# A new step order for pooled attention and a gated feed-forward layer on one core

## The chip, the cores and the metric

The kernel runs on one core of a Trainium2 chip. The core has five engines that run their own streams of instructions and meet through semaphores: TensorE (matmul, with its weight loads apart), VectorE, ScalarE, GpSimd and SyncE, which here issues every DMA. The metric is the device time of one execution in microseconds (us). A short name for an engine in the profile: PE, PEld, DVE, ACT, POOL, SP in the order just given.

## The reference

Attention with pooled keys and values, then a gated feed-forward layer over all tokens. Batch is 8, heads 8, sequence 576, head size 64, so 4608 tokens of width 512; the inner width is 1536.

```
k_p, v_p = mean over 8 neighbours of k, v           # 576 -> 72
attn     = softmax(q k_p^T / 8)                      # 576 x 72 for each head
x        = attn v_p, heads side by side              # 4608 x 512
xn       = x / sqrt(mean(x*x) + 1e-6) * rms_g
out      = (silu(xn w_gate) * (xn w_val)) w_out      # 512 -> 1536 -> 512
```

## The kernel before

Weights come as 64-bit floats and are turned into a high and a low part, each of TensorE's float32r type; a product of two such pairs is three matmuls (high-high, low-high, high-low). Tokens are worked in 9 blocks of 512 (`NB`). Blocks 0 to 2 take plain products: for each of 12 slices `f` of the inner width a gate product, a value product (12 matmuls each), and the output product (12 matmuls). Blocks 3 to 8 go in pairs (3 and 4, 5 and 6, 7 and 8) through a seven-product scheme for 2 by 2 blocks: `product` (line 895) for the first layer and `product2` (line 975) for the second, 6 matmuls per step, with sums of blocks prepared by the other engines and partly stored to HBM and read back.

Nothing loops at run time and no scheduler reorders: with `manual_schedule`, each engine carries out its instructions in the order in which the program issues them, and `run` (line 1109) issues them by one long text, `ORDER` (line 52), of 3315 step names. So each engine's stream is that text with the other engines' steps left out. A name is a code of one or two letters (after `_` for the steps of batches 0 and 1 and of block 0) and indices; `:` gives PSUM banks for the step's results, `/` gives which of two or more buffers it takes. A capital first letter of some codes means the other one of VectorE and GpSimd (`_w`/`_W`, `wf`/`Wf`, `lo`/`Lo`, `fl`/`Fl`), or of VectorE and ScalarE (`_C`/`_D`, `_X`/`_Y`).

Steps that the text below names:

- `_S`, `sc` scores on TensorE; `_M` row maximum, `_E` exponentials, `_R` reciprocal, `_N` scaling of the probabilities on GpSimd (line 468); `_T` transposes of them on TensorE (line 536), `_D` or `_C` the copy out, `_A`, `av` probabilities times values
- `_P`, `_p`, `_r`, `_s`, `_B`, `_n`: squares summed on TensorE (line 652), total, root, its inverse, its spread over partitions (line 676), and the copy that scales block 0
- `_l`, `_a`, `_b`, `_c`, `_d`, `_h`, `_w`/`_W`: a weight's load, its conversion on ScalarE and VectorE, its high part (ScalarE), its low part. The low part on GpSimd goes through `cut` (line 292 in the profile), which makes pieces of 256 columns: 4 of them for a whole slice of the first layer, 2 for half of one or for a slice of the output weights
- block 0: `_m` and `_g`, `_e` the gate and value products, `_u`, `_G`, `_F` their scaling, silu and product, `_i` and `_j`/`_L` high and low part of it, `_o` the output product. `mg`, `me`, `gt`, `vl`, `hi`, `lo`/`Lo`, `mo` are the same for blocks 1 and 2
- `wt`, `wf`, `wh`, `wl`, `ws`: sums of weight blocks for the seven products, split and stored
- pairs: `ys`, `yh`, `yl`/`Yl` token sums and their two parts (`Yl` on GpSimd is 4 pieces), `rl` a weight load, `pr` a product; `fs`/`Fs`, `fh`, `fl`/`Fl`, `ft`, `pm` the same for the second layer

The order text was written by a planner that is not part of the file. It gave every step an engine, a place, banks and buffers.

Of the kernel before, what the change touches and what calls it, by code (L numbers as in the profile page):

```python
# [57 lines left out]
_C011 _E101 _N100 _T010:3 _T031 _v00 _V00 _A001:7/0 _Z01 _Y001 _x01 _D020 _b3 _b2 _c3 _c2 _d2 _h0 _y01 _T012:1 _W0
_A000:5 _Z00 _h2 _W2 _D012 _T032:6 _D010 _v01 _A020:4 _k11 _d3 _h3 _l4 _P00:2 _V01 _C032 _w3 _R101 _A021:1 _v10 _x20
_y20 _A010:3 _x00 _y00 _V10/0 _m000:7 _K11/1 _Y021 _x21 _y21 _Z21 _m010:6 _D031 _l7/0 _a7/1 _b7 _c7 _a4 _Z10 _ld/1 _l6  # L60
_ad/0 _m002 _b4 _Z20 _bd _A011:5 _Y011 _Z11 _d7 _x11 _A030 _x30 _Z30 _cd _c4 _x10 _dd _A031:4 _Z31 _P01 _P02 _P03 _a6
_hd _m012 _N101 _d4 _l9/0 _p _T100:1/1 _T101:2 _q11 _y30 _x31 _b6 _k12 _Wd _y11 _r0 _h7 _D101 _y31 _s0 _B00:5 _h4 _y10
_m011 _m001 _m013 _D100 _a9/0 _m003 _n _W4 _m100:5 Wt0/1 _l8 _Y031 _c6 _d6 _W7 _v11 _a8 _T102 _u0 _G0 _h6 _A100:1/1
_S11:27 _b9 _C102 _c9 _d9 _M110 _h9 _m102 _E110 _b8 _m110 _m112 _M111 _F0 _w9 _m101 _W6 _c8 _i0/1 _L0 Wf00 _d8 _lb/0
_R110 _m111 _K12/1 _A101:4 _ab/1 _X101 _bb _B01:6 _h8 _H01 _cb _m103 _u1 wf01 _db Wf02 _E111 _w8 _G1 _m113 _F1 wh03/0
Wl03 _la _X100 _hb _Wb _lf/0 Wf03 ws03 _e2:0 _o0:7564 _aa _g2:3 _i1/1 _ba _ca _L1 wh02/1 _o1 wl02 _af/0 _u2 _G2 _R111
_bf _cf _F2 _N110 _Q10 wd0 _i2/1 _T110:2/1 _D110 _df _hf _Wf _da _j2 _ha _g3:1 _lc _q12 _e3:0 wh01/0 _V11/0 _u3 _G3
# [5 lines left out]
ws21 _Wg _g6 _u6 _V12/0 _D122 _lk _k20 _v13 _o5 _G6 wh22/1 _F6 _i6/1 _ci _S13:10 _M130 _T120:3 _di wh24/0 Wl24 _D120
_j6 wl22 _M131 _g7 _u7 _hi ws22 _e7 _ak _o6 _K20/1 _bk _ck _G7 _F7 ws24 _E130 _dk _A121:3 _al/1 _bl _cl _ln/1 _an/0
_bn _cn _dl _i7/1 _R130 _dn _E131 _R131 _N131 _A120:2 _Y120 _hn _Wn _j7 _Y121 _g8:1 _u8 _V13/0 _G8 _wi _N130 wd4 _e8:0
_F8 _hl _wl _lj/0 _aj/0 _bj _cj _lm/1 _am/1 _bm _dj _T131:1/1 _o7 _D131 _hk _T130 _D130 _q20 sc20:21 wd2 _Q11/0 _cm
_T132 _D132 _dm _Wk _hj _A130:3 _Y130 Wt3/1 Wf30 _A131 _Y131 Wf31 lv21/0 mx201/1 sb201 _hm _Wj _wm _J11 mx200/1 lk21
pv21/0 _e9 sb200 wh33/0 Wl33 ex201 _lo/0 _i8/1 _L8 _g9:1 _u9 _ga:0 wh31/1 _o8 Wl31 ex200 _Q12/1 Wf32 Wf33 _J12 _Q13/0
ws33 _G9 _F9 ws31 _J13 _i9/0 wh34/0 pk21/1 Wl34 ws34 sm201/0 _ao/1 _bo _co _do _ho wh32/0 _L9 _P10:2 _ea _o9 _Wo _ua
sm200/0 nm200 _Ga _lp/0 _r1 Wl32 zd2 ws32 _Fa _ia/0 lq21 _ap/1 _gb:3 Nm201 tr20/1 _bp _La _s1 _B11:1 wd5 _cp _dp _hp  # L80
_ub _Gb _H11 wt4/0 _B10 _H10 _wp _eb:2 dm20 _Fb _oa sc21:10 wf40 wh41/0 Wl41 _t0 ws41 _t1 _ib/1 _jb wf41 wh43/1 _ob
lk22 Wl43 _t2 ws43 _t3 dp20/0 me10:2 Zt00/1 mg10:3 ev03/0 Wf42 Zt01 Zf00 Zf01 zh03/1 mx210/0 st03 sb210 Zl03 pk22/1
# [1127 lines left out]
```

## Time and profile before

| | us |
|---|---|
| median of 3 runs (lowest, highest) | 978.0 (974.93, 978.25) |
| the profiled execution's own time | 976.88 |
| span of the profile, first to last instruction | 975.1 |
| TensorE matmul busy | 947.5 (97%) |
| VectorE busy | 704.2 (72%) |
| ScalarE busy | 492.9 (51%) |
| GpSimd busy | 490.4 (50%) |

Busy time of TensorE counts a matmul that waits inside the pipeline as busy. The granted clock stands in shares of TensorE's full 2.4 GHz: 1.0 is that level, 0.5 is the level of 1.2 GHz. A row of the chain of waits follows the work that ended last back to the start.

### The profile page before, as it was taken

The page shows a single profiled execution, that of the slowest core. Times are in us where ns is not written, and L with a number is a line of the kernel's source. Part 1 is how long each engine was busy: PE and PEld are TensorE (multiplying, and loading weights), DVE is VectorE, ACT ScalarE, POOL GpSimd, SP SyncE. Part 2 cuts the span into 40 slices and gives each one's busy share as a digit, 9 for nine tenths or more (in the row PEclk, how much of TensorE's full clock was granted, in tenths as well). Part 3 has the DMA queues.
Part 4 walks back from the last instruction along what each step waited for, and adds up shares of the span by engine and source line. Part 5 has one row for each costly group of instructions (what it writes and reads, how often), then busy time and mean ns, then how long its engine had stood idle before and what let it go on. Part 6 is the DMA issues. An engine that isn't in the chain of part 4 may idle for free.

```text
span 975.1 us, 14181 instructions
## 1 busy us (share of the span) xinstructions
PE 947.5 (97%) x4670; PEld 752.2 (77%) x4670; DVE 704.2 (72%) x1134; ACT 492.9 (51%) x929; POOL 490.4 (50%) x618
## 2 busy tenths in 40 slices
PE   7799999999999999999999999999999999999997
PEld 6577677777777877877877777877877778888885
DVE  6989898978787888778787877755565884433333
ACT  5876675645555647555455456242543642213332
POOL 3355637222322324433455788432296894445785
PEclk7789999999999999999999999999999999999999
DMA  9537774665766569878887776768686465767646
GB/s 300 183 137 273 225 247 157 215 204 178 240 204 204 171 182 267 251 231 274 253 248 255 202 253 195 243 184 263 217 257 212 155 219 173 229 189 232 205 141 204
DMA packets 142296, 211.41 MB, mean 217 GB/s; under 512 B 12240, under 2 KB 78288, under 8 KB 140944
## 3 DMA queue, kind: packets, MB, share of 16 engines
q1 hardware_dynamic: 142224, 210.52, 68.8%
q8 instruction: 37, 0.61, 0.3%
q14 instruction: 35, 0.29, 0.1%
HBM read 154.24 MB, written 56.23 MB: 216 GB/s over the span
## 4 chain that ended last, share of the span: by engine, by line
PE 76%; DMA 5%; DVE 5%; POOL 5%; ACT 3%; issue 2%; SPq 1%; DVEq 0%; ACTq 0%; POOLq 0%
PE pxy L895 30%; PE psg L1059 15%; PE pf L975 15%; PE po L1093 7%; PE psx L560 3%; PE pss L478 3%; POOL w L292 2%; DMA pt<-rows 1%; DMA ring<-vs 1%; POOL xp L292 1%; POOL hl L292 1%; DMA ring<-vB 1%; DVE wt L326 1%; PE psr L652 1%; DVE wt L330 1%
## 5 line engine op out<-in xcount | busy, mean ns | idle before, releaser
L895 PE MATMUL pxy<-xp,wp 128*128 128x512 f32 x1512 | 361.1, 391 | 1.5 <-ACT o L1104 0.7
L895 PEld LDWEIGHTS pxy<-xp,wp 128*128 128x128 f32 x1512 | 282.3, 188 | 65.3 <-issue 2.5
L975 PE MATMUL pf<-fp,ring 128*128 128x512 f32 x756 | 189.8, 393 | 3.1 <-DMA ring<-vB 1.6
L1059 PE MATMUL psg<-xh,w 128*128 128x512 f32 x544 | 171.2, 396 | 1.4 <-DVE prob L495 1.0
L975 PEld LDWEIGHTS pf<-fp,ring 128*128 128x128 f32 x756 | 139.6, 188 | 39.6 <-DMA ring<-vs 3.9
L1059 PEld LDWEIGHTS psg<-xh,w 128*128 128x128 f32 x544 | 101.2, 189 | 26.5 <-DVE prob L495 1.4
L1059 PE MATMUL psg<-xl,w 128*128 128x512 f32 x272 | 106.7, 392 | 0.0
L292 POOL TENSOR_TENSOR hl<-act,hh 128x256 fp32r<-128x256 f32 x58 | 49.8, 878 | 111.5 <-ACT hh L1075 102.6
L292 POOL TENSOR_TENSOR fp<-fs,fp 128x256 fp32r<-128x256 f32 x108 | 81.1, 778 | 41.7 <-ACT fp L948 37.9
L292 POOL TENSOR_TENSOR fp<-act,fp 128x256 fp32r<-128x256 f32 x72 | 55.1, 786 | 83.1 <-ACT fp L948 81.8
L1093 PE MATMUL po<-w,hh 128*128 128x512 f32 x288 | 72.9, 390 | 0.0
L292 POOL TENSOR_TENSOR w<-wt,w 128x256 fp32r<-128x256 f32 x50 | 48.7, 1000 | 45.7 <-ACT w L344 45.7
L1093 PEld LDWEIGHTS po<-w,hh 128*128 128x128 f32 x288 | 54.1, 188 | 11.6
L292 POOL TENSOR_TENSOR fp<-hb,fp 128x256 fp32r<-128x256 f32 x68 | 54.5, 828 | 13.9 <-ACT fp L948 13.9
L1059 PEld LDWEIGHTS psg<-xl,w 128*128 128x128 f32 x272 | 51.4, 189 | 11.1
L1154 ACT COPY hb<-pxy 128x512 f32<-128x512 f32 x36 | 21.0, 586 | 72.7 <-PE pxy L895 72.7
L1161 DVE TENSOR_TENSOR u<-u,pxy 128x512 f32<-128x512 f32 x36 | 24.7, 685 | 38.0 <-PE pxy L895 37.8
L948 ACT CAST fp<-act 128x512 fp32r<-128x512 f32 x36 | 22.2, 619 | 58.5 <-DVE act L1162 49.3
L948 ACT CAST fp<-fs 128x512 fp32r<-128x512 f32 x54 | 33.0, 618 | 34.3 <-POOL fs L292 16.7
L1155 DVE TENSOR_TENSOR u<-hb,pxy 128x512 f32<-128x512 f32 x36 | 24.6, 684 | 33.3 <-PE pxy L895 19.7
L292 POOL TENSOR_TENSOR fs<-act,hb 128x256 f32<-128x256 f32 x32 | 23.4, 752 | 50.0 <-DVE act L1162 28.0
L1158 DVE TENSOR_TENSOR hb<-u,pxy 128x512 f32<-128x512 f32 x36 | 24.7, 686 | 29.0 <-PE pxy L895 28.1
(193 smaller groups left out, 1636.0 us busy)
## 6 DMA issues: line engine op xcount, KB each, us to landing
wp<-sum SPq DMA_DIRECT2D x144, 256.0 KB
wp<-blocks SPq DMA_DIRECT2D x108, 256.0 KB
ring<-vs SPq DMA_DIRECT2D x72, 256.0 KB
ring<-vB SPq DMA_DIRECT2D x54, 256.0 KB
sum<-wt SPq DMA_DIRECT2D x48, 256.0 KB
blocks<-w SPq DMA_DIRECT2D x24, 512.0 KB
wx<-w SPq DMA_DIRECT2D x10, 1024.0 KB
v<-vN SPq DMA_DIRECT2D x32, 288.0 KB
```

The source lines that it names most:

```text
L292: getattr(eng, op)(*(x[..., o:o + step] for x in (out, a, b)))
L478: nc.tensor.matmul(s["ps", h][:, t * SP:(t + 1) * SP], s["q"][r, o:o + P], s["pk"][r, :], start=True, stop=True)
L560: nc.tensor.matmul(ps[r, :n], s["pv"][:, r], x, start=True, stop=True)
L895: nc.tensor.matmul(ps[:, :NB], w[:, a, c, :], x[:, b, c, :], start=j == 0 and not more, stop=j == len(todo) - 1, skip_group_check=more)
L948: nc.scalar.copy(y[:, 0], f_source(i, k, j))
L975: nc.tensor.matmul(ps[c], w[:, a, c * P:(c + 1) * P], x[:, b], start=j == 0 and n == 0 and not more, stop=j == HALF - 1 and n == 2, skip_g ...
L1059: nc.tensor.matmul(ps[:, :NB], w[:, c, cols], x[c], start=(j == 0), stop=(j == len(todo) - 1))
L1093: nc.tensor.matmul(po[i][t], x[i, f][:, t * P:(t + 1) * P], w, start=(f == 0 and k == 0), stop=(f == NF - 1 and k == 2))
L1154: cp=lambda i, f: S_.copy(later(i, f), st["XY", i, f, 0]),
L1155: u2=lambda i, f: V.tensor_add(u2(i, f), later(i, f), st["XY", i, f, 1]),
L1158: c2=lambda i, f: V.tensor_sub(later(i, f), u3(i, f), st["XY", i, f, 4]),
L1161: v1=lambda i, f: V.tensor_add(u2(i, f), u2(i, f), st["XY", i, f, 5]),
```

## The change

Only the text `ORDER` is another one. It holds the same 3315 steps; the functions, tiles and shapes stay as they are. The plan behind it keeps the pieces that GpSimd makes of one instruction next to each other, and has no piece without a duration. The places of most steps move by a few, banks and buffers are given anew, and 48 steps change their engine: GpSimd has 300 steps for 309, VectorE 1016 for 1006, ScalarE 695 for 696. TensorE has the same 640, and SyncE the same 675.

The stretch of the text around `_T121` as it was, and as it is:

```diff
-wh11/1 wl11 _ce _de _A110:1 _v20/1 _V20/1 _Y110 ws11 _o3 _A111:1 wh13/0 wd1 _i4/0 Wt2/1 _E120 _g5:0 wh14/1 _R120 Wl14
-ws14 Wf20 _li Wl13 _L4 ws13 _ag _o4 _bg _e6 _he _We Wf21 _u5 _cg _E121 _R121 _dg wf22 _N121 wh12/1 Wl12 _e5:2 ws12 _G5
...
+_bg ws13 _e6 _j4 Wf22 _cg _u5 _o4 _G5 _dg _N121 _hg _F5 _i5/0 _T121:1/1 _j5 _g6:0 wh23/0 Wl23 _We _li _ai ws21 wh22/1
```

GpSimd's own stream there, read out of the two texts:

```
before: N111 wl01 _Wc _Wh wf13 wl11 _L4 _We wf22 _N121 _N120 _Wg wl22
after:  N111 _Wa wf12 wf13 _Wc wl11 _N120 wl21 _N121 _We wl22 _Wg _L6
```

TensorE's own stream, from the third output product of block 0:

```
before: _o2 _g4 _T112 _T111 _e4 _S12 _A110 _o3 _A111 _g5 _o4 _e6 _e5 _T121 _T122 _g6 _o5
after:  _o2 _T110 _T112 _T111 _g4 _A110 _S12 _A111 _e4 _g5 _o3 _e5 _e6 _o4 _T121 _g6 _T122 _o5
```

And earlier, from the first: before `_m103 _m113 _e2 _o0 _g2 _o1`, after `_m103 _g2 _m113 _o0 _e2 _o1`; GpSimd's low parts of weights ahead of it: before `_W4 _W7 _W6 _L0`, after `_W6 _W7 _W4 _W9 _L1`. ScalarE's high part `_h7` stood ahead of `_G0` and stands behind it.

## Rows read from the trace of the kernel before

**Rows 1.** The page, parts 1 and 2: busy time by engine, and TensorE's busy share and granted clock in 40 equal slices.
```profile
PE 947.5 (97%) x4670; PEld 752.2 (77%) x4670; DVE 704.2 (72%) x1134; ACT 492.9 (51%) x929; POOL 490.4 (50%) x618
PE   7799999999999999999999999999999999999997
PEclk7789999999999999999999999999999999999999
```

**Rows 2.** Busy time by stretch: us from the span's start, then PE, PEld, DVE, ACT and POOL busy (instructions), granted clock, DMA share, GB/s.
```profile
0.00:25.00 25.00, 18.67 (x147) 16.97 (x148) 17.46 (x41) 14.52 (x63) 7.53 (x19) 0.73 0.90 297
25.00:50.00 25.00, 19.99 (x103) 13.64 (x101) 21.84 (x36) 22.27 (x62) 10.38 (x13) 0.77 0.58 193
50.00:100.00 50.00, 47.59 (x242) 37.29 (x243) 45.30 (x64) 32.86 (x68) 30.43 (x30) 0.94 0.56 198
100.00:200.00 100.00, 96.30 (x493) 75.68 (x492) 89.84 (x147) 67.64 (x151) 47.80 (x51) 0.98 0.67 211
200.00:300.00 100.00, 100.00 (x540) 78.01 (x539) 85.27 (x164) 53.59 (x101) 25.16 (x34) 1.00 0.67 206
900.00:976.00 76.00, 69.91 (x303) 55.75 (x301) 29.39 (x40) 22.47 (x39) 54.51 (x75) 0.99 0.57 184
```

**Rows 3.** The same view in stretches of 5 us.
```profile
45.00:50.00 5.00, 5.00 (x29) 4.71 (x25) 3.83 (x5) 4.98 (x10) 1.57 (x2) 0.58 0.78 235
50.00:55.00 5.00, 5.00 (x22) 4.35 (x22) 3.59 (x9) 1.21 (x4) 0.10 (x1) 0.50 0.69 256
...
110.00:115.00 5.00, 3.89 (x18) 2.88 (x16) 4.47 (x6) 3.37 (x9) 5.00 (x4) 1.00 0.64 244
115.00:120.00 5.00, 3.85 (x14) 2.97 (x15) 4.17 (x7) 3.30 (x6) 1.72 (x3) 0.75 0.83 261
120.00:125.00 5.00, 5.00 (x31) 3.93 (x31) 3.64 (x5) 2.43 (x6) 3.57 (x5) 0.91 0.99 371
150.00:155.00 5.00, 3.97 (x18) 2.98 (x17) 4.47 (x8) 3.22 (x6) 4.13 (x6) 1.00 0.04 8
```

**Rows 4.** The chain of work that ended last, around 110 us: start, us, what.
```profile
108.87 4.78 POOL w L292 x4
...
114.15 0.90 POOL wsum L766
115.05 1.69 POOL prob L468 x2
...
116.78 0.41 PE pst L536 x2
117.19 4.35 PE psg L1059 x12
```

**Rows 5.** TensorE in order of time: start, us, line, operation, tiles, count, and the idle time before with what ended it.
```profile
113.50 0.39 PE L1059 MATMUL psg<-xl,w 128*128 128x512 f32 x1
115.85 0.63 PE L536 MATMUL pst<-ident,prob 128*72 128x128 f32 x4 [1.96 <-POOL prob L468]
116.78 0.41 PE L536 MATMUL pst<-ident,prob 128*72 128x128 f32 x2 [0.30 <-POOL prob L468]
```

**Rows 6.** GpSimd in order of time, same columns.
```profile
56.21 9.98 POOL L292 TENSOR_TENSOR w<-wt,w 128x256 fp32r<-128x256 f32 x10 [6.10 <-ACT w L344]
...
108.87 5.32 POOL L292 TENSOR_TENSOR w<-wt,w 128x256 fp32r<-128x256 f32 x4 [3.03 <-ACT w L344]
...
120.49 2.82 POOL L292 TENSOR_TENSOR w<-wt,w 128x256 fp32r<-128x256 f32 x4 [3.77 <-ACT w L344]
123.36 0.74 POOL L775 TENSOR_TENSOR wt<-wsum,wt 128x256 fp32r<-128x256 f32 x1
```

**Rows 7.** VectorE in order of time: the two reciprocals (`_R120`, `_R121`) that the scalings `_N120` and `_N121` wait for.
```profile
107.54 0.18 DVE L463 RECIPROCAL early<-early 128x5 f32<-128x5 f32 x1
...
111.84 0.18 DVE L463 RECIPROCAL early<-early 128x5 f32<-128x5 f32 x1
```

**Rows 8.** ScalarE in order of time: the silu `_G0`, a high part of a whole slice of the first layer, and of half of one.
```profile
60.11 0.63 ACT L1037 ACTIVATE act<-act 128x512 f32<-128x512 f32 x1
60.65 1.03 ACT L344 CAST w<-wt 128x1024 fp32r<-128x1024 f32 x1
62.72 0.62 ACT L344 CAST w<-wt 128x512 fp32r<-128x512 f32 x1 [1.04 <-DVE wt L330]
```

**Rows 9.** The chain of work that ended last, in the start-up, and one stretch of plain products at the full clock.
```profile
45.36 6.01 PE psr L652 x30
...
54.57 1.84 PE psb L676 x10
...
299.20 10.88 PE psg L1059 x48
```

**Rows 10.** Groups of ScalarE's instructions: busy us, mean ns | idle before.
```profile
L499 ACT ACT_TABLE_LOAD x26 | 33.4, 1283 | 0.5
```

**Rows 11.** In order of time, at the start of the second pair: GpSimd's `Yl53`, then `Yl54` and `Yl55`, and TensorE's product that reads `Yl54`'s result.
```profile
592.84 2.83 POOL L292 TENSOR_TENSOR xp<-xs_S,xp 128x256 fp32r<-128x256 f32 x4 [1.45 <-ACT xp L861]
...
598.73 7.00 POOL L292 TENSOR_TENSOR xp<-xs_S,xp 128x256 fp32r<-128x256 f32 x8 [1.69 <-ACT xp L861]
...
602.10 1.55 PE L895 MATMUL pxy<-xp,wp 128*128 128x512 f32 x6
```

**Rows 12.** The end of the chain of work that ended last.
```profile
957.03 4.02 DMA ring<-vB
...
970.59 1.37 DVE fu L1005 x2
```

More of the change, by code (lines that the diff above doesn't have):

```diff
@@ L58 @@
[L58 to L67, printed above, removed]
@@ L73 @@
[L73 to L82, printed above, removed]
@@ L158 @@
-Fl341 rl510/5 lq70 pr3b6 v13b va3b rm60:3 rt60 rc60 ft341 rs60 pm341 ft342 pm342 rl502/6 ys53/10 ys54 rl503/7 pr510:3
-Fs345 ft344 pr500 Fl344 fh335/4 Fl335 fh325/7 Fl325 ft343 pm343 ft345 cp50 pr502 fh350/8 rl512/0 ft325 ft335 pm325
-Fs365 pm344 cp51 rl521/4 pm335 rl501/6 rl511/3 Fl350 ft350 qc30 yh53 qc31 sa50 Yl53 fh345/5 qe31/1 qe30/0 Fl345 pr512
-sc70:75 oe31 yh52 yl52 fh352/3 fl352 yh54 ft352 pm350:26 Yl54 sa51 pm345 ft351 pm351 ys55 yh55 mx701/1 sb701 mx700/0
-rl504/2 pr504:4 lk72 ft353 fh353/5 sb700 pk72/0 Yl55 pm352 ex701 pr501:5 Qd31 u250 pr511 u251 sm701/1 fh363/6 pr503:7
@@ new lines @@
+_C030 _h2 _D011 _W2 _T031:1 _D031 _d3 _A021:4 _Y021 _v01 _V01 _x20 _h3 _P00:2 _y01 _y00 _y20 _T032:7 _C032 _A011:5
+_ld/1 _ad/0 _W3 _k11 _K11/0 _bd _m010:6 _m000:7 _l4 _x21 _y21 _v10 _m012 _cd _a4 _b4 _Z21 _Y001 _dd _R101 _Y011 _N101
+_x11 _l7/0 _a7/1 _b7 _c7 _Z20 _c4 _hd _A031:3 _Z31 _A010:4 _A030:1 _x30 _Z30 _P02 _Z10 _d7 _l6 _P03 _y11 _Z11 _P01 _d4
+_R100 _N100 _x10 _a6 _x31 _b6 _y30 _p _m002 _r0 _T100:5/1 _T102 _c6 _y10 _V10/1 _Wd _s0 _h4 _d6 _D102 _l9/0 _T101:2
+_l8 _a9/0 _b9 _Y031 _y31 _m001 _D101 _k12 _c9 _d9 _B00 _h6 _n _m011 _m003 _u0 _a8 _W6 _G0 _m013 Wt0/1 _B01:2 _H01
@@ new lines @@
+_S11:37 _M110 _M111 _m100:0 _K12/0 _h7 _lb/0 _la wd0 _b8 _m110:2 _m102 _D100 _A100:5/1 _E110 _A101:1 Wf00 _k13 _W7 _F0
+_c8 _d8 _X100 _m112 _q12 _i0/1 _j0 _m101 _m111 _ab/1 _bb _m103 _u1 _cb Wf01 _db _W4 _g2:3 _h9 _W9 _E111 _h8 Wf02 _m113
+wh03/0 Wl03 _w8 _G1 _o0:7465 _F1 _aa _lf/0 _i1/0 _L1 _ba _ca ws03 _Y101 _af/0 _bf _e2:0 _u2 _cf _lc _hb _Wb _R110 _df
+wh02/1 _da _G2 _F2 _v11 _hf _Wf _i2/1 _o1 Wl02 _L2 ws02 _g3:1 _e3:0 _lh/0 _ac wh01/0 wl01 ws01 _R111 _V11/1 Wf03 _ha
+_o2 _K13/1 _u3 _G3 _bc _cc _F3 _N110 _T110/0 _ah/1 wh04/0 _bh _ch _dc _dh _N111 _T112:3 _D110 _le _T111:1 Wl04 _Wa
@@ new lines @@
+Wt1/0 _i3/0 _j3 Wf10 _D112 _D111 _g4:0 _u4 _v12 _A110:1 _hh Wf11 wf12 _Y110 _v20/1 _S12:23 _wh _ae _A111:1 _e4:0 _Y111
+_M120 _M121 _be _ce wf13 _hc _g5:1 _Wc _G4 _F4 ws04 wh11/0 wl11 _lg wh14/1 Wl14 ws14 _V20/1 _E120 _R120 _N120 _o3
+_V12/0 Wt2/1 _de _Q11/0 _E121 _R121 ws11 wh12/1 Wl12 ws12 Wf20 _i4/1 Wf21 _e5:2 wh13/0 _ag _he Wl13 _q13 wh21/1 wl21
+_bg ws13 _e6 _j4 Wf22 _cg _u5 _o4 _G5 _dg _N121 _hg _F5 _i5/0 _T121:1/1 _j5 _g6:0 wh23/0 Wl23 _We _li _ai ws21 wh22/1
+Wf23 _u6 _G6 _T122:2 _o5 _bi wl22 _lk _D122 _F6 _Wg _k20 _C121 ws23 _ci _T120:2 wh24/0 ws22 Wl24 _D120 _K20/0 _i6/1
@@ new lines @@
+_L6 _Q10 _J11 _S13:10 _ll/0 _M131 _A121:3 _X121 _di _ak _al/1 _hi _g7 _u7 _bk _G7 _M130 _bl _cl ws24 _o6 _ln/1 _an/0
+_bn _cn _E130 _Wi _dn _e7:2 _A120:3 _Y120 _g8:1 _dl _v13 _F7 _i7/0 _L7 _ck _e8:2 _dk _u8 _E131 _R131 _N131 _R130 _lm/1
+_V13/0 _hn _wn _o7 _G8 _T131/1 _hl _F8 _wl _lj/0 _aj/0 _bj _cj _q20 _N130 _T130:1 _am/1 _bm _D131 _T132:3 _dj _hj _cm
+_dm _i8/0 lv21/0 _D130 _D132 zd3 Wt3/1 Wf30 _hm sc20:02 mx201/0 _A130:1 _Y130 _Wm _wj _A131:3 _hk lk21 pv21/0 _L8
+_Q12/1 Wf31 wh31/1 _g9:1 _Y131 _lo/0 _e9 wh33/0 Wl31 ws31 _Q13/0 Wf32 Wf33 Wl33 _u9 _G9 mx200/1 _o8 sb200 _F9 _Wk ws33
@@ new lines @@
+cp50 Fl325 pr502 ft344 ft345 fh335/4 Fl335 Fs365 yh53 Fl345 ft325 pm325 pm344 ys54 sa50 qe31/1 ft335 qe30/0 pm335 qc31
+fh365/7 qc30 yh52 yh54 rl510/5 pr510:3 cp51 ft352 yl52 pm345 sc70:75 fh350/5 Yl53 fh352/3 oe31 ys55 yh55 pr512 sa51
+rl513/7 rl505/4 mx701/0 mx700/0 pr504:4 rl501/5 sb701 sb700 ft350 ft351 Fl350 pm350:26 pm351 lk72 pk72/0 fh361/5 oe30
+Yl54 ex701 pr501:5 ft353 fh353/6 fl352 pm352 ft354 Qd31 qf31/1 pr511 rl520/6 rl503/2 rl521/3 u250 Yl55 pr503:5 u350
+lv70/0 c250 rl514/0 fh354/8 u251 Fl353 pm353 ft361 pr505:7 v250 Qd30 qf30/0 ys56 Fl354 lq71 fh355/4 Fl355 pm354
@@ new lines @@
+sc73:10 Jn71 Fs532 mx730/1 mx731/0 sb731 qb50 rl595/2 rl593/0 av720:3 xc720 sq72/0 Fs540 pr593:6 Fl531 sb730 rl596/4
+ft521 rl592/7 pr592 u359 pr595:0 c259 v259 ft522 rl5b4/3 rl5a0/1 pr5a0:3 lv73/1 pv73/1 fh532/8 rl5a3/0 ex730 pr596
+rl5b1/7 sm730/1 pr5a3:6 Fl521 Nm730 fh522/7 Fl522 ex731 sm731/1 sw59 vb59 pm521 Fs561 Fl532 Fs562 rl5a1/2 pr5a1:7
+ft530 v159 rl5a6/4 pm522 cp5a rl5a2/5 pr5a2 rl5a4/6 Nm731 Fs533 sa5a u25a u35a pr5a4:6 Jn72 fh533/7 tr73/0 c25a
+rl5b0/1 rl5a5/2 pr5a5:1 Fs543 sa59 v25a pm530 rl5b3/5 dm73 ft523 fh543/4 sw5a va59 Fl533 Fs563 pr5a6 ft524 ft532
@@ L227 @@
+Fl762 fh754/8 Fl754 fl753 pm753 Qd70 fh760/7 qf70/1 pm754 Fl760 qc71 Qd71 qf71/0 ft761 pm760 fh761/6 ft762 ft764
+fh763/5 pm755 ft763 qg71 og71 of71 Fl761 pm761 pm762 of70 fs765 Fs764 fh764/4 Fl763 pm763 Fl764 qg70 ft765 pm764 og70
+fh765/3 Fl765 pm765 qh71 oh71 qh70 oh70
 """
```

288 lines of the change are left out of this document (141 added, 147 removed).

## Prediction

> **What bounds the kernel now.** I read the page first: TensorE is busy 947.5 of 975.1 us, every other engine at most 72%, and the granted clock is below full only in the first two of the forty slices [rows 1]. So TensorE's own work is the bound, and a new order can only touch what TensorE idles and what it does at half clock. The busy time by stretch says where that is [rows 2]: the idle time is 25.00 - 18.67 = 6.3 us up to 25, 5.0 up to 50, 2.4 up to 100, 3.7 up to 200 and none up to 300. From 900 to 975.1 it is 75.1 - 69.9 = 5.2, of which 975.1 - 970.59 = 4.5 follow the last sum's start [rows 12]. The whole is 27.6, so 300 to 900 holds the other 27.6 - 22.6 = 5.0. From 120 us on an order can win no more than these 5.0, some 0.7 ahead of the tail, and the 3.7 less the 1.11 and 1.15 idle from 110 to 120 [rows 3], together 7; the rest is the start.
>
> Then I took the same view in short stretches and the chain [rows 3, 4]. Two places stand out. From 45.4 to 55 the engine is busy, at a clock of 0.50 to 0.58: thirty of the small sums of squares take 6.01 us [rows 9]. At 115 the chain leaves TensorE, goes through GpSimd (four pieces, `_We`; then 0.90, `wf22`; then two scalings in 1.69), and comes back at the transposes `_T121` and `_T122` [rows 4]. TensorE waits 1.96 and 0.30 us there for the scalings [rows 5], and the granted clock falls from 1.00 to 0.75 in that stretch [rows 3]. The next gate product takes 4.35 us [rows 4], where 48 matmuls of the kind at full clock take 10.88 us, so 12 take 2.72 [rows 9].
>
> **The change part by part.** *The stall at `_T121`.* Its reciprocal was done at 111.84 + 0.18 = 112.0 [rows 7], and yet the scaling `_N121` began at 115.05 [rows 4], because `_We` (108.87 to 114.2, beginning late by a wait for its high part [rows 6]) and `wf22` were ahead of it on GpSimd. In the new order `_N120`, `wl21`, `_N121` stand ahead of `_We`, and `wf22` has gone to VectorE. The set of TensorE's steps ahead of `_T121` is the same, so TensorE comes there at about the same time: 113.50 + 0.39 = 113.9 [rows 5]. What it finds hangs on `wl21`, a new wait in front of `_N121`: it takes 0.74 [rows 6], and needs a high part on ScalarE that now stands behind some whole-slice conversions of about 1.03 each [rows 8]. Queued behind it on GpSimd are `_N121`, `_We` and `wl22`, and TensorE's `_T121` waits for the first. With `_N120` begun behind its reciprocal (107.72) and 1.69 / 2 = 0.85 a scaling, `_N121` could end at 112.0 + 0.85 = 112.9; with two of those conversions and `wl21` in front, at 112.9 + 2.06 = 115.0. The first removes the whole stall: 1.96 + 0.30 and the half-clock loss 4.35 - 2.72 = 1.63, together 3.9 us. The second leaves a wait of 1.1 and probably part of the clock loss. Below nothing it could go if the high part came later still, but then the wait is the one of today. I take 3.4, near the better end, as VectorE has six steps fewer ahead of `_R121` and these run at 0.75 us each or so (4.47 for 6 in 110 to 115 [rows 3]). The bounds are 0 and 3.9. `_We` now ends later, about 113 + 5.3; its readers stand behind `_g6` as before, in products that run past 120.
>
> *The start, up to 60 us.* The order of some forty steps of VectorE and ScalarE changes. Both are the bound there: 21.84 and 22.27 of the 25 us from 25 to 50 [rows 2]. Counted in the two texts, 87 VectorE steps stand ahead of `_F0`, the first finished slice, where there were 85; at the mean of that stretch, 21.84 / 36 = 0.61, that is up to 1.2 us more. But the ones taken out are larger than those put in by their shapes (two copies to the transposed attention and a cast, for three short copies, a set of pooled keys and a sum), so I take +0.5. ScalarE exchanges `_h7` (half a slice, 0.62 [rows 8]) and three copies for `_h6` (1.03) and three others ahead of `_G0`, about +0.2. Later slices come some tenths earlier, as `_F1` and `_F4` have less VectorE work ahead. I put the start at 0, with bounds -1 and +3; the half-clock stretch is the reason for a wider one, and a rival.
>
> *The low parts of `_g2`'s weights.* On GpSimd `_W4` and `_W6` change places. Ten pieces took 9.98 us from 56.21 [rows 6]. Before, `_W4` was the first four, over by 60.2; now it is the last four, over at 66.2 if the ten start as before. `_g2` stands one product earlier on TensorE, at about 66.7 by my walk along the order. So the cover is half a us: I count nothing, and a rival below pays for it. `_W9` comes onto GpSimd ahead of the low part `_L1` (two pieces, 2 us at that pace).
>
> *150 to 155.* `_e9` and `_g9` change places where TensorE idles 5.00 - 3.97 = 1.03 [rows 3]; it lies between 0 and 1.0 of gain, and I take 0, as what both wait for is the same weight and state of VectorE and ScalarE.
>
> *The pairs.* `Yl53` ends at 592.84 + 2.83; `Yl54` and `Yl55` follow at 598.73 for 7.00, and the product that reads `Yl54` starts at 602.10, just as its half is there (598.73 + 3.50 = 602.2) [rows 11]. In the new order that product stands one product earlier, and GpSimd has a low part `Fl` ahead of `Yl53` and one between it and `Yl54`. Gain 0, loss up to three such products, 3 x 1.55 = 4.7; I take 0, since GpSimd idles 1.45 and 1.69 there, about what the added parts of four pieces in 2.8 take.
>
> *Edits with no price of their own.* From 200 to 300 TensorE idles nothing, with VectorE at 85.27, ScalarE at 53.59 and GpSimd at 25.16 of 100 us [rows 2]: the engine changes of single steps are covered there. Each switch of ScalarE's table costs 1.283 us [rows 10]; counted along the text there are 83 for 80, so 3.8 us more, on an engine that is half idle [rows 1]. Banks and buffers: their first users stand at about the same distance. The tail has the same four products last, behind the same read-back of 4.02 us [rows 12], and stays.
>
> *A rule against the change.* The same four-piece operation took 5.32 us at 108.87 and 2.82 at 120.49 [rows 6], the first beside a VectorE busy 4.47 of 5 us, the second beside 3.64 [rows 3]. The Trainium skill, "GPSIMD Engine Reference", section "8. Key points", says that GpSimd shares its SBUF interfaces with VectorE and is held up by VectorE instructions in certain modes or with two SBUF inputs. The rows agree with that as far as they go. By the rule, pieces set next to each other slip by up to 5.32 - 2.82 = 2.5 us per group where VectorE is dense; by the rows alone they may slip or not, and the sum keeps its values. That is behind the second and third rivals.
>
> *The sum.* The profiled execution took 976.88 by its own time, 1.8 over its span. Start 0, `_T121` -3.4, the rest 0: 973.5. The median of the runs is 978.0, 1.1 above that execution; so the forecast is 974.6.
>
> **The rivals.**
>
> *More is won.* The stretch at half clock, 45.4 to 55.4, holds nearly 10 us, of which at full clock up to 5 would be left. If the earlier sums of squares come closer to the other work ahead of them, part of it runs at full clock; 3.4 for `_T121` and 4.6 here give 978.0 - 8 = 970. For it: the step order there is altered, and the clock has two levels, so it goes by jumps. Against it: these sums stand behind VectorE's and ScalarE's copies, which are no shorter.
>
> *Nothing changes in sum.* The stall at `_T121` goes, and `_e5`, `_T122` or the `Yl` stretch meets it again: low parts slip by one group's 2.5 us plus 1 us, 978.0 - 3.4 + 3.4 = 978. For it: at 602 the margin was 0.1 us; after 113 `_We` is late by as much as `_N121` is early. Against it: TensorE never idles from 200 to 300 in the same density.
>
> *Slower.* `_W4` comes last of GpSimd's ten pieces while `_g2` comes earlier. Behind `_W6`, `_W7` waits for `_h7`, which now stands behind `_G0` (60.11 + 0.63, then 0.62 [rows 8]: ready at 61.4 at the earliest); when that slips with the start, `_W4` slips with it. Then TensorE waits at 66.7 and the chain moves on to `_L1` behind `_W9`. A slip of 4.5 and two fallings of the clock at 1.7 each (1.63 at `_T121`) cost 7.9; with `_T121`'s 3.4 kept, 978.0 + 7.9 - 3.4 = 982.5. It decides from where `_W4` ends beyond 66.7 + 1.7 = 68.4. For it: half a us of cover. Against it: `_W6`'s high part needs only VectorE steps that come no later, and four of the ten pieces may run at 0.7 us.
>
> *The change does not do what it says.* If most order moves are covered, and `wl21`'s wait is as long as `_We`'s was, the time is 978.0 again; this is inside the second case.
>
> **How the numbers follow.** The forecast has 0.42, more gain 0.24 (around 970), nothing in sum 0.18 (around 978), slower 0.16 (982.5 and above). A difference of 0.5%, 4.9 us, is about what a measurement of this kernel can tell from no change: faster means below 973.1, slower above 982.9. The forecast lies 1.5 inside the bound, so about a third of its chance (0.14) is faster, and all of the gain case: 0.38. Of the slower case and the other cases' upper ends 0.16 lies above. The rest, 0.46, is between. The range: below, the gain case to its middle and 2 further, 968; above, the slower case just beyond its price, 983. The forecast's own range takes in `_T121`'s bounds and the start's better one: 974.6 - 0.5 - 1.0 to 974.6 + 3.4, 973 to 978.
>
> **What would show it.** For `_T121`: the wait for the scaling ahead of its transposes below 0.5 us, a granted clock of 1.00 from 115 to 120, and the gate product after it at 2.7. For the start: the first plain products at the same place within a us, the thirty sums of squares in 6.0 us. For `_W4`: no idle time with a GpSimd low part as its releaser between 64 and 72. For the pairs: no wait of a product for `xp` from GpSimd at about 600. The prediction is wrong if the half-clock stretch before 60 us grows or shrinks by more than 2 us, if a wait of over 2 us for a GpSimd piece appears anywhere, or if `_T121` still waits.

## The result, and the profile after

The changed kernel takes 981.9 us in the median of 13 runs (979.5 to 989.1), the kernel before 977.4 (974.5 to 981.0). Over all runs the ratio is 1.0053 (that of the medians is 1.0046), with an interval of 1.0035 to 1.0070. It became about 5 us slower where 3.4 less were forecast; 981.9 lies inside the range, at its upper end, with the wrong sign. The profiled execution took 980.02 us by its own time, 3.1 more than that of before.

The five longest of the 13 runs (983.2 to 989.1, 986.0 in the mean) have a granted clock of 0.976 to 0.978, the other eight (980.7 in the mean, 3.3 above the kernel before) one of 0.980 to 0.984. By these clocks, 0.977 and 0.982 in the mean, the five were granted some 0.005 x 980 = 5 us less of TensorE's full clock; that estimate is about their whole distance of 5.3. The trace below is of one of the eight and doesn't show where they lose it.

Busy time and granted clock on the page of the changed kernel, as in [rows 1]:

```profile
PE 947.0 (97%) x4670; PEld 748.5 (77%) x4670; DVE 712.6 (73%) x1144; ACT 497.9 (51%) x931; POOL 500.7 (51%) x611
PE   7898999999999999999999999999999999999997
PEclk7799999999999999999999999999999999999999
```

TensorE is busy as long as before, so the difference between the two traces is idle time. Where it lies is read from the busy time by stretch, with the columns of [rows 2] and [rows 3]:

```profile
80.00:100.00 20.00, 18.52 (x102) 14.14 (x101) 19.21 (x27) 13.52 (x29) 16.29 (x16) 1.00 0.59 201
100.00:110.00 10.00, 8.63 (x39) 6.81 (x37) 8.47 (x13) 6.74 (x24) 6.30 (x4) 1.00 0.45 142
110.00:115.00 5.00, 4.69 (x23) 3.86 (x24) 4.10 (x6) 2.22 (x4) 4.75 (x4) 1.00 0.66 245
115.00:120.00 5.00, 4.43 (x21) 3.40 (x20) 4.23 (x7) 3.87 (x7) 3.40 (x5) 1.00 0.88 328
140.00:160.00 20.00, 17.93 (x101) 13.93 (x100) 19.52 (x31) 13.30 (x25) 12.27 (x13) 1.00 0.61 188
...
300.00:900.00 600.00, 593.60 (x2845) 472.97 (x2844) 418.75 (x653) 282.47 (x452) 307.22 (x390) 1.00 0.74 224
900.00:978.00 78.00, 70.36 (x304) 56.14 (x302) 29.30 (x39) 21.57 (x38) 54.26 (x73) 1.00 0.56 174
```

From 110 to 120 TensorE idles 0.88 us where it idled 1.11 + 1.15, and the clock is 1.00 where it was 0.75 [rows 3]. But from 80 to 110 it now idles 1.48 + 1.37 = 2.85, and nothing in that stretch before:

```profile
80.00:100.00 20.00, 20.00 (x108) 16.06 (x108) 19.39 (x25) 11.54 (x18) 12.36 (x12) 1.00 0.75 271
100.00:110.00 10.00, 10.00 (x45) 7.49 (x44) 9.93 (x15) 8.41 (x28) 5.64 (x7) 1.00 0.65 188
```

VectorE, nearly full there before (19.39 + 9.93 = 29.3 of 30 us), is busy 27.7 now. From 140 to 160 TensorE idles 2.07, where 150 to 155 had 1.03 [rows 3]. From 300 to 900 it is 6.4 for 5.0, and from 900 to the end at 977.9 it is 77.9 - 70.4 = 7.5 for 5.2 [rows 2]. The same for the changed kernel in TensorE's order of time, only instructions from 75 us on with idle time ahead of them, and what ended it (columns of [rows 5]):

```profile
75.69 0.73 PE L1093 MATMUL po<-w,hl 128*128 128x512 f32 x2 [0.93 <-POOL hl L292]
86.97 1.25 PE L536 MATMUL pst<-ident,prob 128*72 128x128 f32 x10 [0.56 <-POOL prob L468]
94.72 0.73 PE L1059 MATMUL psg<-xh,w 128*128 128x512 f32 x2 [0.90 <-DVE act L1033]
110.31 1.20 PE L1093 MATMUL po<-w,hl 128*128 128x512 f32 x4 [1.68 <-DVE hl L292]
117.31 1.19 PE L1093 MATMUL po<-w,hl 128*128 128x512 f32 x4 [0.57 <-DVE hl L292]
142.29 0.85 PE L536 MATMUL pst<-ident,prob 128*72 128x128 f32 x6 [0.57 <-POOL prob L468]
145.89 1.19 PE L560 MATMUL psx<-pt,pv 72*64 72x288 f32 x8 [1.48 <-ACT pt L542]
...
592.55 1.65 PE L895 MATMUL pxy<-xp,wp 128*128 128x512 f32 x6 [1.54 <-ACT act L1156]
...
956.59 11.57 PE L975 MATMUL pf<-fp,ring 128*128 128x512 f32 x48 [1.76 <-DMA ring<-vs]
```

The first of these rows, in `_o1`, is no new wait (0.93 before too), but a place to compare: it stands at 75.69 to 77.01 in the eight traces with the changed order up to there, and at 77.21 to 80.33 in six with the order of before. So the changed kernel leads at this row and loses the lead behind it; and one order alone spreads over 3 us here, so that the lead of a single trace says little.

The 1.96 at `_T121` [rows 5] is gone. The 1.68 at 110.31 stands in its place: `_o4` waits for `_j4`, the low part that was on GpSimd as `_L4` and is on VectorE now. Two of GpSimd's rows and the chain of waits tell why `_j4` is late; first GpSimd in order of time:

```profile
101.44 3.93 POOL L775 TENSOR_TENSOR wt<-wsum,wt 128x256 fp32r<-128x256 f32 x1
...
111.15 1.77 POOL L468 TENSOR_TENSOR prob<-prob,early 128x360 f32<-128x360 f32 x1
```

and the chain that ended last (start, us, what):

```profile
101.48 3.90 POOL wt L775
...
105.40 2.02 DMA sum<-wt
...
107.49 0.41 ACT wt L771
107.90 0.49 ACT wt L318
...
108.83 1.04 ACT w L344
109.87 0.32 ACT wt L771
```

`wl11`, an instruction of 0.74 us elsewhere [rows 6], takes 3.9. Its store lands 2.0 later and frees the buffer for `wh13` on ScalarE (L771); `Wl13` on VectorE waits for `wh13`, and `_bg` and `_j4` stand behind `Wl13`. Behind `wh13` on ScalarE come `_ag`, `_he` and `wh21`, and for `wh21` the `wl21` that the change puts ahead of `_N121`. The prediction had seen that last wait alone. The row at 592.55 is new as well, and comes back below.

### The profile page after: what moved, and what is told of

It is laid out like the page before. It is cut to its first block, busy times and chain, and to the rows that moved or that the text cites. A ratio compares the mean times of both kernels' runs of the same rounds, so it can differ in the third digit from the quotient of the medians.

```text
span 977.9 us, 14177 instructions
## 1 busy us (share of the span) xinstructions
PE 947.0 (97%) x4670; PEld 748.5 (77%) x4670; DVE 712.6 (73%) x1144; ACT 497.9 (51%) x931; POOL 500.7 (51%) x611
## 4 chain that ended last, share of the span: by engine, by line
PE 72%; DVE 6%; DMA 6%; POOL 3%; issue 2%; ACT 2%; SPq 0%; DVEq 0%; ACTq 0%; POOLq 0%
PE pxy L895 32%; PE pf L975 14%; PE psg L1059 13%; PE po L1093 7%; PE psx L560 3%; PE pss L478 3%; DMA ring<-vB 2%; DMA ring<-vs 1%; POOL w L292 1%; DMA wp<-blocks 1%; DVE xraw L644 1%; DMA sum<-wt 1%; DVE acc L637 1%; POOL hl L292 1%; DVE wt L330 0%
## 5 line engine op out<-in xcount | busy, mean ns | idle before, releaser
L292 POOL TENSOR_TENSOR hl<-act,hh 128x256 fp32r<-128x256 f32 x58 | 52.6, 928 | 127.8 <-ACT hh L1075 119.6
L292 POOL TENSOR_TENSOR w<-wt,w 128x256 fp32r<-128x256 f32 x60 | 62.1, 1063 | 18.3 <-ACT w L344 18.3
L292 POOL TENSOR_TENSOR fp<-hb,fp 128x256 fp32r<-128x256 f32 x68 | 56.8, 862 | 9.6 <-ACT fp L948 9.1
L1161 DVE TENSOR_TENSOR u<-u,pxy 128x512 f32<-128x512 f32 x36 | 24.5, 684 | 45.1 <-PE pxy L895 45.0
L1156 ACT ACTIVATE act<-pxy 128x512 f32<-128x512 f32 x36 | 21.4, 598 | 52.1 <-PE pxy L895 46.9
L1157 DVE TENSOR_TENSOR u<-u,pxy 128x512 f32<-128x512 f32 x36 | 24.6, 683 | 30.7 <-PE pxy L895 30.3
L1093 PE MATMUL po<-w,hl 128*128 128x512 f32 x144 | 42.2, 403 | 4.7 <-DVE hl L292 2.6
```

The costliest lines, as they stand in the source:

```text
L292: getattr(eng, op)(*(x[..., o:o + step] for x in (out, a, b)))
L1093: nc.tensor.matmul(po[i][t], x[i, f][:, t * P:(t + 1) * P], w, start=(f == 0 and k == 0), stop=(f == NF - 1 and k == 2))
L1156: sa=lambda i, f: S_.activation(new_act(i, f), st["XY", i, f, 0], AF.Silu),
L1157: u3=lambda i, f: V.tensor_add(u3(i, f), u2(i, f), st["XY", i, f, 3]),
L1161: v1=lambda i, f: V.tensor_add(u2(i, f), u2(i, f), st["XY", i, f, 5]),
```

## The experiments

The time of the kernel before, 977.4, turns ratios into us; each interval holds 95%. A mixture keeps the first steps of one order and takes the rest in the sequence, and with the engines, of the other. The text `ORDER` of the mixtures and edits has fewer lines, so their line numbers are 3 or 4 lower.

**Which part loses?**

```diff
-ORDER = before
+ORDER = after                                        # c_after
+ORDER = after[:192] + rest of before                 # ab192
+ORDER = after[:709] + rest of before                 # ab709
+ORDER = before[:709] + rest of after                 # ba709
+ORDER = before[:192] + after to 1017 + rest of before   # bab
+ORDER = after[:192] + before to 1017 + rest of after    # aba
+ORDER = before[:1017] + rest of after                # ba1017
```

c_after: 

> The changed kernel as it is, timed beside the three mixtures below. Its profile: a lead of 4 us over the kernel before at 60 us, given back in small waits up to 185 us and in the tail. Theory REST (the 5 us are lost behind 185 us, above all in the tail's loads; the start is a real gain): 980 to 982, and the spread of its executions (979.5 to 989 so far) comes from the loads late in the kernel. Theory START (the start is what is unsteady: in some executions TensorE is granted half clock for longer before 60 us): 980 to 982 too, with the slow executions those of a low mean granted clock (0.976 to 0.978 against 0.984).

ab192: 

> The first 192 steps (to about 47 us) in the order of the changed kernel, everything behind them in the order of before. REST: the lead of the start stays, 977.4 - 4 = 973 to 974, steady. START: slow and spread like the changed kernel, 979 to 982, with a mean clock between 0.976 and 0.984.

ab709: 

> The first 709 steps (to about 185 us) in the changed order, the rest in the order of before. REST: -4.2 of the start, +3.4 - 3.1 + 1.8 in the waits from 70 to 160 us, so 977.4 - 2 = 975 to 976. START: as the changed kernel without its tail (+1.7), 979 to 980, spread.

ba709: 

> The first 709 steps in the order of before, the rest in the changed one. REST: +1.5 of small waits up to 900 us and +1.7 in the tail, 977.4 + 3 = 980 to 981. START: 977.4 + 1 to 2 = 978 to 979, steady, with the clock of before.

c_after measured 1.0042 (1.0024 to 1.0059); its runs lie between 978.8 and 984.6 at clocks of 0.980 to 0.984, and the longest has 0.980 like two of the shorter ones. So START finds nothing in these 12 runs, but its sign is in the 13 of the result, whose five longest have the lowest clocks. That the start differs from one execution to the next the traces show: up to 70 us the granted clock is 0.78 in that of before, 0.73 in ba1017's and 0.80 in ba1017_tail's, which have the same order there. Where the five long runs lost their clock stays open. ab192 is at 0.9987 (0.9965 to 1.0008), -1.3 us, between the numbers of REST and START: the changed start shows neither a loss nor a clear gain. The mixtures at 709 took 1.0086 (1.0057 to 1.0116) and 1.0106 (1.0080 to 1.0132), more than either whole and outside what both theories gave. The seam shows in both of them, in TensorE's order of time, first of ab709, then of ba709:

```profile
210.51 1.90 PE L557 MATMUL psx<-pt,pv 72*64 72x256 f32 x8 [4.11 <-DMA pt<-rows]
```
```profile
208.60 2.19 PE L556 MATMUL psx<-pt,pv 72*64 72x256 f32 x8 [3.98 <-DMA pt<-rows]
```

A transfer is late where the two orders meet, and from 185 to 220 us the granted clock is 0.90 in the one and 0.85 in the other. Neither kernel has this wait, and both have a clock of 1.00 there; so these two tell nothing of the parts. The seams at 192 and 1017 show no such wait.

bab: 

> Steps 1 to 192 and from 1018 on in the order of before, and only those between (about 47 to 275 us) in the changed order. If the middle is what loses (small waits from 80 to 185 us, 12 us of loss against 9.5): 977.4 + 2.5 = 980, with the new waits of the changed kernel in its profile (o4 behind _j4, pt at 146 us). If the loss lies behind 275 us (tail and the pairs): 977 to 977.5.

aba: 

> The changed kernel with the middle (steps between 192 and 1017, about 47 to 275 us) in the order of before. If the middle is what loses, as its mixture into the kernel before (+3.4) says: 981 - 3.4 = 977.6. If the parts do not add up, because a lead or a lag at the seams is taken up by waits that are there anyway: between 976 and 980.

ba1017: 

> The kernel before up to step 1017 (about 275 us), the changed order behind it. If the parts add up: start -1.2 (ab192), middle +3.4 (bab), start and rest together +1.7 (aba), so the rest alone is 1.7 + 1.2 = +2.9, 980.2. If only the middle loses: 977.3.

bab took 1.0035 (1.0018 to 1.0053), aba 1.0017 (1.0003 to 1.0031), ba1017 1.0025 (1.0011 to 1.0039): start -1.3, middle +3.4, rest +2.4, in sum +4.5 against +4.1 and +5.2 for the whole; and start and rest without the middle are -1.3 + 2.4 = +1.1 against +1.7. The parts add up within their intervals. The middle is the largest by these values, though its interval (+1.8 to +5.2) overlaps that of the rest (+1.1 to +3.8). In aba the wait at `_T121` is back:

```profile
114.29 0.73 PE L532 MATMUL pst<-ident,prob 128*72 128x128 f32 x4 [1.96 <-POOL prob L464]
```

**What was the stall at T121 worth?** Three kernels from the one before; GpSimd's stream:

```diff
-_L4 _We wf22 _N121 _N120
+_N120 _L4 _N121 _We wf22      # b_swap
+_L4 _N120 _N121 _We wf22      # b_swap2
+_L4 _N120 wf22 _N121 _We      # b_swap3
```

b_swap: 

> The kernel before with GpSimd's order at T121 alone as the change has it: N120 straight behind its reciprocal, N121 ahead of the four pieces of We, wf22 behind them; wl21 stays on VectorE. Theory SUM (the stall was worth what the prediction said and a wait taken away is time won): no wait for the scaling at T121, 977.4 - 3.4 = 974. Theory TURN (between 80 and 185 us VectorE, ScalarE and GpSimd set the pace, and a wait taken away at one place comes back at the next): T121 waits for nothing, but We is late by 4 us and what reads it or wf22 waits; 976 to 977.5.

It took 1.0022 (1.0000 to 1.0043), 979.6, above what both theories gave. `_N120` waits for its reciprocal, and `_L4`, queued behind it, ends later than TensorE can use; the wait for it, in TensorE's order of time:

```profile
106.78 2.10 PE L1089 MATMUL po<-w,hl 128*128 128x512 f32 x4 [3.54 <-POOL hl L288]
```

b_swap2: 

> The kernel before once more with the scalings ahead of We, but with GpSimd's low part L4 left ahead of both (L4, N120, N121, We, wf22), since L4 behind N120 made TensorE wait 3.54 us for it in b_swap. SUM: no wait at T121 and none for L4, 977.5 - 3.4 = 974. TURN: both waits are gone, and up to 3 us appear at other places between 100 and 130 us (We's readers, g5, e5, o5); 976 to 978.

It took 1.0045 (1.0029 to 1.0062), 981.8, above both again. TensorE, and then VectorE, in order of time:

```profile
119.09 1.22 PE L1056 MATMUL psg<-xh,w 128*128 128x512 f32 x2 [3.80 <-DVE act L1068]
```
```profile
118.02 0.42 DVE L763 TENSOR_TENSOR wsum<-wsum 128x256 f32<-128x256 f32 x1 [3.35 <-POOL wsum L763]
```

`wf22` behind `_We` holds up `Wf23` on VectorE by 3.35 us. `_F5`, which reads the PSUM bank that `_g6` needs, stands behind `Wf23`.

b_swap3: 

> The kernel before with We alone behind the scalings: GpSimd's order is L4, N120, wf22, N121, We. In b_swap2 the wait for the scaling was gone, but TensorE idled 3.80 us ahead of g6, since Wf23 on VectorE waited for wf22 behind We, and F5 behind Wf23. SUM: with wf22 in front nothing waits there, 977.3 - 3.4 = 974. TURN: another wait of 1.5 us or more shows between 105 and 130 us, 976 to 978.

It took 0.9989 (0.9972 to 1.0007), -1.1 us, and the interval takes in no change. That is in TURN's range, though the wait that shows is less than TURN's 1.5. What is left of the wait, and the next one:

```profile
114.05 0.85 PE L533 MATMUL pst<-ident,prob 128*72 128x128 f32 x6 [0.20 <-POOL prob L465]
115.80 0.74 PE L1056 MATMUL psg<-xh,w 128*128 128x512 f32 x2 [0.90 <-DVE act L1068]
```

So none of the three had the stall's 3.9 us whole: `_F5` is late for `_g6` by 0.90 even in the best of them. A gain of 3.4 lies outside the interval (-2.7 to +0.7).

ab_swap3, the same behind the changed start:

```diff
-before[:192]
+after[:192]
```

> The same, with the first 192 steps from the changed kernel (ab192 was at 0.9987, -1.2 us). SUM: 977.3 - 1.2 - 3.4 = 972.7, clear of both kernels. TURN: 975 to 976, as ab192.

It took 0.9971 (0.9957 to 0.9986), 974.5 us: below both kernels, and 1.4 to 4.2 us below the one before by its interval. It lies near the sum -1.3 - 1.1 = -2.4 of the two parts as measured, and half a us below TURN's numbers; SUM's -1.2 - 3.4 = -4.6 is outside.

**Can the changed kernel's waits be mended one by one?**

```diff
-_i4/1 Wf21 _e5:2 wh13/0 _ag _he Wl13 _q13 wh21/1 wl21 _bg ws13 _e6 _j4
+_i4/1 Wf21 _j4 _e5:2 wh13/0 _ag _he Wl13 _q13 wh21/1 wl21 _bg ws13 _e6     # a_j4, a_all
-_R121 ws11
+_R121 _N121 ws11                                     # a_all: N121 from behind wl21
-_dj _hj _cm _dm _i8/0 lv21/0 _D130 _D132
+_dj _D130 _D132 _hj _cm _dm _i8/0 lv21/0             # a_D130, a_all
-wl11
+Wl11                                                 # a_wl11: on VectorE
```

a_j4: 

> The changed kernel with one step moved: the low part _j4 on VectorE stands right behind Wf21, ahead of Wl13 and _bg, which wait for ScalarE. SUM: the wait of 1.68 us ahead of the output product _o4 goes, 981.4 - 1.7 = 979.7. TURN: that wait goes, but TensorE now comes 1.7 us earlier to T121, where N121 ends at 112.25 behind wl21, so 1.3 of it come back as a wait for the scaling: 981 and no difference that shows.

It took 1.0038 (1.0020 to 1.0055), as TURN had it. The wait at `_o4` is gone, and `_T121` waits 2.20, more than before the change:

```profile
114.99 0.63 PE L532 MATMUL pst<-ident,prob 128*72 128x128 f32 x4 [2.20 <-POOL prob L464]
```

c_after shows the same without an edit. In its trace `wl11` took 0.75, the instruction behind it 3.94, TensorE idled 0.29 ahead of `_T121` and not at all ahead of `_o4`, and the execution took 980.01, as the one with the 1.68 did.

a_wl11: 

> The changed kernel with the low part wl11 on VectorE in place of GpSimd, where it took 3.93 us of which 0.74 are its own and stood at the head of the chain wl11, its store, wh13, wh21, wl21, N121. SUM: the chain is 3 us shorter, o4's wait of 1.68 goes and T121 doesn't wait; 981 - 1.7 to 2 = 979 to 979.5. TURN: N120, next on GpSimd, takes the 3.9 in its place, as in c_after, and 980 to 981 stays.

It took 1.0032 (1.0019 to 1.0045), whose lower end is SUM's number. GpSimd's next instruction, `_N120`, has the 3.93 now, though it alone takes 0.85 to 0.97; TURN had said so:

```profile
103.54 3.93 POOL L464 TENSOR_TENSOR prob<-prob,early 128x360 f32<-128x360 f32 x1 [0.70 <-DVE early L459]
```

TensorE's waits there, in order of time, are another set:

```profile
110.14 1.19 PE L1089 MATMUL po<-w,hl 128*128 128x512 f32 x4 [0.34 <-DVE hl L288]
113.99 0.63 PE L532 MATMUL pst<-ident,prob 128*72 128x128 f32 x4 [0.83 <-POOL prob L464]
123.88 0.71 PE L556 MATMUL psx<-pt,pv 72*64 72x288 f32 x4 [1.81 <-ACT pt L538]
```

a_D130: 

> The changed kernel with the copies D130 and D132 on ScalarE ahead of the high part hj, which waits for VectorE. Theory CLOCK (the waits of 0.57 and 1.48 us close together at 142 to 146 sometimes bring TensorE to half clock, as in c_after and in the mixture of the middle, where the granted clock of 140 to 160 was 0.91): the 1.48 goes, the clock there is 1.00, and the median falls by 1.5 to 3, 978 to 979.5. TURN: the wait goes and g9 or e9 waits instead, 980.5 to 981.

It took 1.0043 (1.0023 to 1.0062): no gain. The 1.48 is gone and 0.99 come back at the next product:

```profile
146.87 0.73 PE L1055 MATMUL psg<-xh,w 128*128 128x512 f32 x2 [0.99 <-ACT xraw L579]
```

The clock that CLOCK was after is in c_after's busy time by stretch. It costs at most 0.09 x 20 = 1.8 us there and nothing in the first profile of the same kernel (1.00); a_D130's trace has 1.00 too, and its time is no lower:

```profile
140.00:160.00 20.00, 17.84 (x93) 13.50 (x92) 18.78 (x30) 12.50 (x23) 12.24 (x14) 0.91 0.64 193
```

a_all: 

> The changed kernel with all waits mended that its trace names: _j4 behind Wf21, N121 straight behind its reciprocal ahead of wl21, D130 and D132 ahead of hj, and the stores of the tail behind the loads. SUM: -1.7 at o4, -2.2 at T121 (as it came back in a_j4), -1.5 at A130, -1.5 in the tail, from 981: 975 to 977. TURN: 979 to 980.

It took 1.0026 (1.0012 to 1.0039), in TURN's range: of about 7 us of waits mended, 1.6 show against c_after and 2.6 against the 1.0053, with intervals that overlap. TensorE waits 2.02 for copies on ScalarE at a place that had no wait:

```profile
123.40 0.71 PE L556 MATMUL psx<-pt,pv 72*64 72x288 f32 x4 [2.02 <-ACT pt L538]
```

**The tail.** SyncE's order in the changed kernel, and with the stores behind the loads:

```diff
-oe71 ft751 ft752 ft753 oe70
+ft751 ft752 ft753 oe71 oe70              # a_tail, ba1017_tail, a_all
...
-ft763 og71 of71 of70 ft765 og70
+ft763 ft765 og71 of71 of70 og70          # a_tail, ba1017_tail, a_all
...
-ft753 oe70 ft754 of71 ft760 ft755
+ft753 ft754 ft760 ft755 oe70 of71        # best2, on ab_swap3
```

a_tail: 

> The changed kernel with SyncE's order in the tail alone altered: the load ft751 ahead of the store oe71, the load ft765 ahead of the stores og71, of71 and of70. If the stores ahead of the loads are what makes them late: the waits for ft751 (1.8 us) and ft765 (0.5) go or halve, 981.4 - 1.5 to 2 = 979.5 to 980. If the loads are late by what else is on the rings: no change, 981.4.

ba1017_tail: 

> The same with the stores of the tail behind the loads, as in a_tail. If the rest's loss is the tail's waits (2.3 us in the changed kernel's trace after 940 us against 0.55 in a_tail): 1.5 to 2 below ba1017, 978.5. If it is small waits from 300 to 900 us: as ba1017, 980.

The changed kernel's queue (start, us, transfers) and its wait of 1.76 above go together: the store of `c_1e` stands between the loads.

```profile
950.82 0.34 SPq L1010 DMA_DIRECT2D outT<-c_1e  x1
951.58 1.68 SPq L963 DMA_DIRECT2D ring<-vs  x3
...
967.06 0.47 SPq L1010 DMA_DIRECT2D outT<-c_0f  x1
967.63 0.40 SPq L963 DMA_DIRECT2D ring<-vB  x1
```

In a_tail the waits for loads in the last 40 us are two, for 2.76 in the changed kernel (0.20 + 0.30 + 1.76 + 0.34 + 0.16):

```profile
957.99 4.53 PE L971 MATMUL pf<-fp,ring 128*128 128x512 f32 x18 [0.28 <-DMA ring<-vs]
962.79 11.57 PE L971 MATMUL pf<-fp,ring 128*128 128x512 f32 x48 [0.27 <-DMA ring<-vs]
```

Its time didn't move, 1.0040 (1.0024 to 1.0057). Behind the order of before the same edit did: 0.9995 (0.9976 to 1.0013) against 1.0025 for ba1017, -2.9 us, give or take 2.3 by the two intervals. By the traces it is worth 2.2 in the one and 2.14 - 1.19 = 0.95 in the other (the sums of waits for loads after 940; before has 1.25). That stores ahead of loads go with late loads is in both pairs of traces; its size in the times lies between 0 and 3, and whether the tail is the whole of the rest's loss stays open.

It need not be, for the rest has a second new wait. The product at 592.55, at the start of the second pair, waits 1.52 to 1.56 us for ScalarE's silu in all eleven traces with the changed rest. The nine with the rest of before don't have it; they have 0.46 to 1.08 a little later, ahead of the scores. In the trace of before:

```profile
596.20 1.33 PE L478 MATMUL pss<-pk,q 64*128 64x72 f32 x18 [0.46 <-ACT c_0e L997]
```

No run took this wait alone away.

best2: 

> ab_swap3 (0.9971 of before) with the stores oe70 and of71 of the tail behind the loads ft754, ft760 and ft755. If stores ahead of loads slow the loads here too: the wait of 0.95 us for ft760's transfer (4.02 us in the trace of before) falls below 0.4, and the time is 0.5 to 0.8 below ab_swap3, 974. If that load is late by the loads beside it: as ab_swap3, 974.5.

It took 1.0037 (1.0015 to 1.0058), 6 us more than ab_swap3. The store `of71` frees the buffer of the next result, so `qf70` on VectorE waits 6.10 for it, and TensorE 3.72 for `qf70`; VectorE, then TensorE, in order of time:

```profile
960.88 0.69 DVE L996 TENSOR_TENSOR c_0f<-fu,pf 128x512 f32<-128x512 f32 x1 [6.10 <-DMA outT<-c_1f]
```
```profile
961.66 11.74 PE L972 MATMUL pf<-fp,ring 128*128 128x512 f32 x42 [3.72 <-DVE c_0f L996]
```

So both expectations missed: the load's 0.95 is gone from the trace, and the late buffer costs 3.72 in its place.

## Why the prediction was wrong

*The stall at `_T121`, -3.4.* The stall is gone and the clock stays at 1.00 from 115 to 120, as asked of the profile. That is luck in part: TensorE comes there late, behind the 1.68 at `_o4`, and without that wait `_T121` waits 2.20 (a_j4). In the prediction's own sum for the later end of `_N121`, 112.9 + 2.06, the 0.74 of `wl21` is left out; with it the wait would have been 1.8, nearly that of before. The term was mis-sized besides. The nearest move by itself, the two scalings ahead of `_We`, gives -1.1 (b_swap3), and +2.2 or +4.4 when one neighbour on GpSimd is put on the wrong side (b_swap, b_swap2). The prediction counted steps ahead of `_N121`; it didn't ask what waits next once TensorE comes there 2 us earlier (`_F5` for `_g6`).

*"The rest 0".* This step failed most. The middle loses 3.4 (bab) with the stall's gain in it. Between 80 and 185 us the prediction had a term for `_T121` and one for 150 to 155, and put the other moves there at nothing without a reason: that single changes of engine are covered it said of 200 to 300 us, where TensorE idles nothing. VectorE is busy 85.27 of 100 us in that stretch [rows 2], but 29.3 of 30 from 80 to 110. The time was lost in front of waits, in the one trace `_j4` behind `Wl13` behind `wh13` behind a store. So full an engine has no room for a blocked instruction at its head, and each repair was followed by another wait within 15 us. The traces of a_j4, a_wl11 and a_D130 show that, as TURN has it; c_after's 1.0042 lies inside the intervals of all three, which also leave room for a gain of a us or two. Which of the moved steps would have to go back for the whole 3.4 is not shown.

*The rival "nothing changes in sum"* came nearest: the stall goes and its time comes back as waits behind late low parts, at a price of 3.4. The places were others (80 to 110, `_o4` and 140 to 160 for `_e5`, `_T122` and the `Yl` stretch), and the size, by the values measured, was 3.4 + 1.1 = 4.5, the middle's loss and the stall's worth.

*A rule against the change.* The Trainium skill, "GPSIMD Engine Reference", section "8. Key points", was weighed, with a slip of 2.5 for a group of pieces, and put behind the rivals. The traces of the changed middle agree with it as far as they go, on single instructions: one of 0.74 took 3.93.

*The tail "stays".* Wrong: the last four products are the same, but `ft765` went behind three stores and `ft751` behind one, and the prediction didn't count the queue. TensorE's waits for loads after 940 went from 1.25 to 2.76 (1.95 in c_after).

*The start, 0 with -1 and +3.* It holds within its interval: -1.3 (-3.4 to +0.8). The time at half clock moved: it is 30 to 40 now (0.50), and 45 to 55, at 0.58 and 0.50 before [rows 3], has 0.92 and 0.74. The thirty sums of squares took 3.5 us in this trace where 6.0 was asked for. The whole did not change, for up to 70 us the clock is 0.78 in both traces:

```profile
0.00:70.00 70.00, 61.20 (x362) 46.30 (x363) 60.76 (x107) 53.80 (x167) 36.36 (x46) 0.78 0.71 235
```

*`_W4`, the pairs, the tables.* No wait for a GpSimd low part of a weight shows from 64 to 72, so the rival on the slower side had the sign and not the cause. `Yl54` and `Yl55` start at 598.57 for 598.73 [rows 11] and no product waits for them, as forecast. But the pairs are not at 0: a product there waits 1.54 for ScalarE's silu (the row at 592.55), where the prediction looked at GpSimd alone. ScalarE loads 83 tables for 80, as counted; what that costs no run shows.

Of the signs that the prediction named for being wrong, this trace has none at `_T121`, no wait of TensorE over 2 us for a GpSimd piece, and up to 70 us the same time at half clock. They were set where the prediction had put a price, and the loss lay beside these places.

## What to carry to other kernels

A wait in the chain is worth its length less what the next engine in line is late by behind it: before a stall is counted as gain, walk the buffers and banks behind it with TensorE early. In an order written by a planner, look at every instruction that can block at the head of a nearly full engine, and at stores in the same queue as loads in both directions: a store ahead delays a load, a store behind delays the buffer it frees. And mixtures of two orders, cut where both have done nearly the same steps, show which part loses; look first whether the cut itself makes a wait, and weigh the parts by many runs, since the start of one order differed by 3 us between traces.
